# One attention step for each chunk between the first large products: next scores, output, state, in place of two half steps

## The chip, the cores and the metric

The kernel runs on one core of a Trainium2 chip. The metric is the device time of one execution in microseconds (us), lower is better. A profile is one execution recorded by the hardware profiler; its span runs from the first to the last instruction.

Five engines work side by side, each through its own queue in order: PE (TensorE, matrix products), DVE (VectorE), ACT (ScalarE), POOL (GpSimd) and SP (SyncE, which here issues the loads). They wait for each other through semaphores.

## What is computed

Three parts in a row, all in float32 (2 batches, 8 heads, 768 positions, 64 channels a head; 1536 tokens of 512 features afterwards):

```python
# 1: attention with decay, block by block, with a running state for each head
intra = (q_b @ k_b.T * Dmask) @ v_b
inter = (q_b * lam ** (pos + 1)) @ state
out_b = intra + inter
state = lam ** block * state + (k_b * lam ** (block - 1 - pos)).T @ v_b
# 2: first feed-forward
h = x @ w_in                      # 512 -> 2048
g = where(h >= 1, h, where(h <= -1, 0, (h + 1) ** 2 / 4))
x = g @ w_out
# 3: second feed-forward
x = ((x @ w_a) * (x @ w_b)) @ w_out2   # 512 -> 1536 -> 512
```

## The kernel before

The attention works on chunks of 128 positions, twelve of them (six for each batch; `CPB` is 6). Chunk `c` goes through four functions:

- `att_scores(c)`: eight small products of keys and queries on PE (line 131), into two PSUM banks.
- `att_mask(c)`: POOL scales the keys (`kd`, line 143) and the queries (`qd`, line 160), DVE multiplies the scores by the decay mask into two tiles `pm` (line 152).
- `att_state(c)`: eight products of `kd` and values on PE (line 173); POOL lets the old state decay (line 185) and DVE adds the new part (line 188; for the first chunk of a batch a copy, line 183). The last chunk of a batch (5 and 11) needs none.
- `att_out(c)`: state times `qd` (line 199, not for the first chunk of a batch) and values times `pm` (line 203) on PE into one bank. ACT and DVE write the result as a rounded part and a rest (lines 215 and 216) into `x`, which the first large product reads.

All large products go through `mm3` (line 277): float32 values stand as two rounded parts, so each product is three matmuls. The tokens are worked on in three blocks of 512, four chunks each, kept as `x` and later `y`. `h_bank(j, block)` is a product of twelve matmuls with its activation: ACT starts it (296), DVE goes on (297, 298), and ACT and POOL split it into the two parts of `g` (288, 289). Weights come as 64-bit numbers and are turned into two parts on the core by `split_w`: ACT (256, 260), DVE (257, 261, 264, 267), ACT and POOL again (288, 289).

Chunks 0 to 3 come first, in an order written out by hand. The scores and the mask of chunk 4 follow. From there a list of half steps is worked off between the first large products, two half steps after each `h_bank` of blocks 0 and 1, and three after the fourth. A half step is either "scores of the next chunk, state of this one" or "mask of the next chunk, output of this one, loads of the one after". Chunks 4 to 7 make `x` of block 1, which the fifth `h_bank` reads; chunks 8 to 11 make `x` of block 2. Outside the part written by hand, a scheduler sets the order of instructions on each engine at build time. Where the text says bank 0, 1, ... it means the `h_bank` calls in their order: 0 to 3 read block 0, 4 to 7 block 1.

Of the kernel before, what the change touches and what calls it, by code (L numbers as in the profile page):

```python
# [18 lines left out]
NCHUNK = B * S // CH  # L19
# [15 lines left out]
def retention_ffn_kernel(ctx: ExitStack, tc: tile.TileContext, lam, att, w1i, w1o, w2ab, w2o, out):  # L35
# [18 lines left out]
    def bank():  # L54
        return ps_p.tile([128, 512], F32, tag="ps", name="ps")

    def t2(name):
        return t2_p.tile([128, 512], F32, tag="t2", name=name)
# [55 lines left out]
    ck = {}  # L114
    sc = {}
    pm = {}
    kd = {}
    qd = {}

    def load_chunk(c, parts=(0, 1, 2, 3)):  # L120
        t = ck.setdefault(c, [None] * 4)
        for i in parts:
            t[i] = acc_p.tile([128, 512], F32, tag="acc", name=("qT", "kT", "kn", "vn")[i])
            nc.sync.dma_start(out=t[i], in_=att[c, i])

    def att_scores(c):
        qT, kT = ck[c][:2]
        sc[c] = [bank(), bank()]
        for h in range(H):
            p0, pr = 64 * (h % 2), h // 2  # L130
            nc.tensor.matmul(  # L131
                out=sc[c][h % 2][:, pr * CH:(pr + 1) * CH],
                lhsT=kT[p0:p0 + 64, pr * CH:(pr + 1) * CH],
                rhs=qT[p0:p0 + 64, pr * CH:(pr + 1) * CH],
                start=True,
                stop=True,
            )

    def att_mask(c):
        cc = c % CPB  # L140
        if cc < CPB - 1:
            kd[c] = t2("kd")
            (nc.vector if c == 0 else nc.gpsimd).tensor_tensor(  # L143
                out=kd[c].rearrange("p (a e d) -> p a e d", a=H // 2, e=2),
                in0=ck[c][2].rearrange("p (a e d) -> p a e d", a=H // 2, e=2),
                in1=dmask[:, :, CH - 1:CH].rearrange("p (a e) i -> p a e i", e=2).to_broadcast([128, H // 2, 2, D]),
                op=ALU.mult,
            )
        pm[c] = []
        for i in range(2):  # L150
            p = t2("pm")
            nc.vector.tensor_tensor(  # L152
                out=p.rearrange("p (a i) -> p a i", a=H // 2), in0=sc[c][i].rearrange("p (a i) -> p a i", a=H // 2),
                in1=dmask.rearrange("p (a e) i -> p e a i", e=2)[:, i], op=ALU.mult,
            )
            pm[c].append(p)
        del sc[c]
        if cc:
            qd[c] = t2("qd")
            (nc.vector if c == 3 else nc.gpsimd).tensor_tensor(  # L160
                out=qd[c], in0=ck[c][0], in1=tabq.rearrange("p a i -> p (a i)"), op=ALU.mult
            )

    def att_state(c):
        cc = c % CPB
        if cc == CPB - 1:
            return
        u = bank()
        k = kd.pop(c)

        for h in range(H):
            p0, pr = 64 * (h % 2), h // 2
            nc.tensor.matmul(  # L173
                out=u[p0:p0 + 64, pr * D:(pr + 1) * D],
                lhsT=k[:, h * D:(h + 1) * D],
                rhs=ck[c][3][:, h * D:(h + 1) * D],
                start=True,
                stop=True,
            )
        u4 = u[:, 0:H // 2 * D].rearrange("p (a e) -> p a e", a=H // 2)  # L180
        old, new = st[cc % 3], st[(cc + 1) % 3]
        if cc == 0:
            nc.vector.tensor_copy(new, u4)
        else:
            nc.gpsimd.tensor_tensor(
                out=new, in0=old, in1=tabq[:, :, CH - 1:CH].to_broadcast([128, H // 2, D]), op=ALU.mult
            )
            nc.vector.tensor_tensor(out=new, in0=new, in1=u4, op=ALU.add)

    def att_out(c):  # L190
        cc = c % CPB
        o = bank()
        s = st[cc % 3]
        pairs = [(pr, slice(pr * 128, (pr + 1) * 128)) for pr in range(H // 2)]
        if cc:
            for pr, cols in pairs:
                for e in range(2):
                    r = slice(64 * e, 64 * e + 64)
                    nc.tensor.matmul(out=o[r, cols], lhsT=s[r, pr, :], rhs=qd[c][r, cols], start=(pr == 0), stop=False)  # L199
        for pr, cols in pairs:  # L200
            for e in range(2):
                h = 2 * pr + e
                nc.tensor.matmul(  # L203
                    out=o[64 * e:64 * e + 64, cols],
                    lhsT=ck[c][3][:, h * D:(h + 1) * D],
                    rhs=pm[c][e][:, pr * CH:(pr + 1) * CH],
                    start=(cc == 0 and pr == 0),
                    stop=(pr == H // 2 - 1),
                )
        nb, t0 = c // 4, (c % 4) * CH  # L210
        if nb not in xy:
            xy[nb] = xy_p.tile([128, 2, KT, TB], F32R, tag="xy", name="x")
        o4 = o.rearrange("p (a i) -> p a i", a=KT)
        hi, lo = (xy[nb][:, i, :, t0:t0 + CH] for i in range(2))
        nc.scalar.copy(hi, o4)  # L215
        nc.vector.tensor_tensor(out=lo, in0=o4, in1=hi.bitcast(F32), op=ALU.subtract)  # L216
        for d in (ck, pm, qd):
            d.pop(c, None)


# [72 lines left out]
    def h_bank(ft, nb):  # L293
        ps = product_in("1i", ft, nb)
        r = t2("r")
        nc.scalar.activation(out=r, in_=ps, func=ACTF.Relu, scale=0.5, bias=half)  # L296
        nc.vector.scalar_tensor_tensor(out=r, in0=r, scalar=1.0, in1=r, op0=ALU.min, op1=ALU.mult)  # L297
        nc.vector.tensor_tensor(out=r, in0=r, in1=ps, op=ALU.max)
        g = g_p.tile([128, 2, 512], F32R, tag="g", name="g")
        split_act(r, g[:, 0], g[:, 1])  # L300
        gt[1, ft, nb] = g

    def ab_bank(ft, nb):
        pa = product_in("2i", 2 * ft, nb)
        a = t2("a")
        nc.scalar.copy(a, pa)  # L306
        pb = product_in("2i", 2 * ft + 1, nb)
        nc.vector.tensor_tensor(out=a, in0=a, in1=pb, op=ALU.mult)
        g = g_p.tile([128, 2, 512], F32R, tag="g", name="g")
        split_act(a, g[:, 0], g[:, 1])  # L310
        gt[2, ft, nb] = g
# [39 lines left out]
    with tc.manual_schedule(engines={mybir.EngineType.SP, mybir.EngineType.PE}):  # L351
# [19 lines left out]
        att_state(0)  # L371
        att_mask(1)
        att_out(0)
        att_state(1)
        att_scores(3)
        att_mask(2)
        att_out(1)
        att_state(2)
        split_w()
        att_mask(3)  # L380
        att_out(2)
        att_state(3)
        load_chunk(4)
# [4 lines left out]

    att_scores(4)
    att_mask(4)  # L390
    queue = [(c, half_way) for c in range(4, NCHUNK) for half_way in range(2)]

    def att_step():
        if not queue:
            return
        c, half_way = queue.pop(0)
        if not half_way:
            if c + 1 < NCHUNK:
                att_scores(c + 1)
            att_state(c)  # L400
        else:
            if c + 1 < NCHUNK:
                att_mask(c + 1)
            att_out(c)
            if c + 2 < NCHUNK:
                load_chunk(c + 2)

    def ahead(used):

        while nxt["split"] < min(used, len(order)):  # L410
            split_w()
# [4 lines left out]
    def second(s):  # L416
        f, g, nb = s
        last = g == (FF1 // 512 if f == 1 else FF2 // 256) - 1
        for m in range(4):
            if f == 1:  # L420
                y_bank(g, nb, m, last)
            else:
                o_bank(g, nb, m, last, 2 if last and nb == NB - 1 and m == 3 else 1)
            extra()
# [3 lines left out]
    def extra():  # L428
        if todo:
            todo.pop(0)()  # L430

    for i, s in enumerate(stages):
        f, g, nb = s
        if f == 1:
            base = 8 * g
            plan = {0: base + 7, 1: base + 10, 2: base + 12}
        else:
            base = 8 * (FF1 // 512) + 6 * g
            plan = {0: base + 6, 1: base + 8, 2: base + 10}
        need = plan[nb]  # L440
        if i == 0:
            ahead(4)
        todo.extend([split_w] * max(0, need - nxt["split"] - len(todo)))
        if f == 1:
            for j in range(4):
                h_bank(4 * g + j, nb)
                for _ in range(3 if (i, j) == (0, 3) else 2):
                    att_step()
                extra()
        else:  # L450
            for j in range(2):
                ab_bank(2 * g + j, nb)
                extra()
        if i:
            second(stages[i - 1])
# [47 lines left out]
```

## Time and profile before

| | |
|---|---|
| median of 3 runs | 631.24 us (629.97, 631.24, 631.33) |
| profiled execution | 629.82 us, span 628.0 us |
| mean granted clock of PE in it | 0.988 of full |
| PE busy | 610.6 us, 97% of the span |
| DVE, ACT, POOL busy | 375.7, 247.6, 246.5 us |

The shares are those of the whole span. The attention with the first large products lies in its first 92 us.

### The profile page before, as it was taken

Reading aid. Unit: us, or ns where it says so; the run is one execution under the profiler, and the core shown is the slowest. Engines: PE = TensorE matmul, PEld = TensorE weight load, DVE = VectorE, ACT = ScalarE, POOL = GpSimd, SP = SyncE. Lnnn points to the kernel's source line nnn. Section 1 sums busy time; section 2 is a strip of 40 time slices with the busy share of each in tenths; the row PEclk is TensorE's granted clock in tenths of the full one; section 3 lists DMA queues with packets and bytes.
Section 4 is the critical chain, followed back from the end, with each engine's and each line's share of the span. In section 5 each row is a group of like instructions: output and inputs, shape, how many; then the busy total and the mean of one; then the engine's idle time right before and its main releaser. Section 6 shows DMA issues by size and latency. Waiting matters only on the chain.

```text
span 628.0 us, 8231 instructions
## 1 busy us (share of the span) xinstructions
PE 610.6 (97%) x3171; PEld 501.9 (80%) x3172; DVE 375.7 (60%) x558; ACT 247.6 (39%) x421; POOL 246.5 (39%) x196
## 2 busy tenths in 40 slices
PE   5889899999999999999999999999999999999998
PEld 2768678888888888888888888888888888888886
DVE  0899792585787788679743333555555555555324
ACT  0344344455345435435453455333333333333110
POOL 1756662443352454335675333333322223333210
PEclk9899899999999999999999999999999999999999
DMA  6997210211111122123111221111121111210013
GB/s 192 390 335 261 64 63 24 68 67 68 67 68 55 67 80 68 33 68 101 52 49 34 68 67 68 67 68 67 68 68 67 55 57 58 67 34 1 1 67 135
DMA packets 20503, 52.71 MB, mean 84 GB/s; under 512 B 2408, under 2 KB 4208, under 8 KB 20464
## 3 DMA queue, kind: packets, MB, share of 16 engines
q1 hardware_dynamic: 20448, 52.18, 24.3%
q8 instruction: 25, 0.41, 0.3%
q14 instruction: 14, 0.11, 0.1%
q10 hardware_dynamic: 16, 0.00, 0.0%
HBM read 49.02 MB, written 3.15 MB: 83 GB/s over the span
## 4 chain that ended last, share of the span: by engine, by line
PE 93%; DMA 3%; DVE 2%; POOL 1%; issue 1%; ACT 0%; SPq 0%; DVEq 0%; POOLq 0%
PE ps L277 89%; PE ps L203 2%; PE ps L199 1%; PE ps L131 1%; DMA raw<-in_w1i 1%; DMA tabq<-rows 1%; DMA lamp<-in_lam 1%; PE ps L173 1%; DMA rows<-base 0%; POOL base L90 0%; DVE pm L152 0%; DVE v L261 0%; POOL kd L143 0%; POOL qd L160 0%; DVE x L216 0%
## 5 line engine op out<-in xcount | busy, mean ns | idle before, releaser
L277 PE MATMUL ps<-y,win 128*128 128x512 f32 x864 | 198.8, 389 | 0.0
L277 PEld LDWEIGHTS ps<-y,win 128*128 128x128 f32 x864 | 162.2, 188 | 33.6
L277 PE MATMUL ps<-x,win 128*128 128x512 f32 x576 | 137.1, 396 | 2.3 <-ACT x L215 1.8
L277 PE MATMUL ps<-g,wout 128*128 128x512 f32 x576 | 132.6, 389 | 0.0
L277 PEld LDWEIGHTS ps<-x,win 128*128 128x128 f32 x576 | 109.0, 190 | 26.6 <-ACT x L215 1.9
L277 PEld LDWEIGHTS ps<-g,wout 128*128 128x128 f32 x576 | 108.1, 188 | 22.5 <-issue 0.2
L289 POOL TENSOR_TENSOR win<-v,win 128x512 fp32r<-128x512 f32 x40 | 52.7, 1317 | 151.0 <-ACT win L288 151.0
L277 PE MATMUL ps<-wout,g 128*128 128x512 f32 (+1 forms) x438 | 100.7, 386 | 0.0
L289 POOL TENSOR_TENSOR g<-r,g 128x512 fp32r<-128x512 f32 x48 | 66.5, 1385 | 86.1 <-ACT g L288 60.8
L257 DVE TENSOR_SCALAR hc<-hc 128x512 f32<-128x512 f32 x68 | 36.9, 542 | 102.2 <-ACT hc L256 102.2
L277 PEld LDWEIGHTS ps<-wout,g 128*128 128x128 f32 x438 | 81.6, 188 | 16.7
L321 DVE TENSOR_TENSOR acc<-acc,ps 128x512 f32<-128x512 f32 (+1 forms) x97 | 64.8, 679 | 47.6 <-PE ps L277 47.5
L289 POOL TENSOR_TENSOR wout<-v,wout 128x512 fp32r<-128x512 f32 x28 | 36.7, 1312 | 85.2 <-ACT wout L288 85.0
L264 DVE SCALAR_TENSOR_TENSOR v<-raw,v 128x512 int32<-128x512 int32 x68 | 68.0, 1000 | 2.2
L297 DVE SCALAR_TENSOR_TENSOR r<-r 128x512 f32<-128x512 f32 x48 | 37.7, 786 | 50.3 <-ACT r L296 50.2
L267 DVE CUSTOM_DVE_ANT_0 v<-v,c 128x1024 uint16<-128x1024 uint16 x68 | 55.6, 818 | 6.3
L306 ACT COPY a<-ps 128x512 f32<-128x512 f32 x36 | 21.1, 587 | 95.3 <-PE ps L277 94.0
L288 ACT CAST win<-v 128x512 fp32r<-128x512 f32 x40 | 24.9, 621 | 84.7 <-DVE v L267 84.7
L289 POOL TENSOR_TENSOR g<-a,g 128x512 fp32r<-128x512 f32 x36 | 46.5, 1291 | 25.8 <-ACT g L288 25.8
L296 ACT ACTIVATE r<-ps,half 128x512 f32<-128x512 f32 x48 | 32.8, 684 | 47.2 <-PE ps L277 47.2
L261 DVE TENSOR_SCALAR v<-hc 128x512 int32<-128x512 int32 x68 | 44.5, 654 | 4.3
L256 ACT ACTIVATE hc<-raw 128x512 f32<-128x512 f32 x68 | 45.3, 665 | 2.0 <-DMA raw<-in_w1i 2.0
(45 smaller groups left out, 375.2 us busy)
## 6 DMA issues: line engine op xcount, KB each, us to landing
raw<-in_w2ab SPq DMA_DIRECT2D x24, 512.0 KB, 3.2
raw<-in_w1i SPq DMA_DIRECT2D x16, 512.0 KB, 3.3
raw<-in_w1o SPq DMA_DIRECT2D x16, 512.0 KB, 3.3
raw<-in_w2o SPq DMA_DIRECT2D x12, 512.0 KB, 3.4
qT<-in_att SPq DMA_DIRECT2D x12, 256.0 KB, 4.8
kT<-in_att SPq DMA_DIRECT2D x12, 256.0 KB, 5.0
kn<-in_att SPq DMA_DIRECT2D x12, 256.0 KB, 5.5
vn<-in_att SPq DMA_DIRECT2D x12, 256.0 KB, 5.7
```

Of the source, the lines that this page charges most:

```text
L256: nc.scalar.activation(out=hc.bitcast(F32), in_=high.bitcast(F32), func=ACTF.Abs)
L257: nc.vector.tensor_scalar(out=hc.bitcast(F32), in0=hc.bitcast(F32), scalar1=HIGH_MIN, scalar2=HIGH_MAX, op0=ALU.max, op1=ALU.min)
L261: nc.vector.tensor_scalar(out=v, in0=hc, scalar1=3, scalar2=0x3FFFFFFF, op0=ALU.logical_shift_left, op1=ALU.bitwise_and)
L264: nc.vector.scalar_tensor_tensor(out=v, in0=high, scalar=-0x40000000, in1=v, op0=ALU.bitwise_and, op1=ALU.bitwise_or)
L267: nc.vector.tensor_tensor(out=v, in0=v, in1=c, op=ALU.add)
L277: nc.tensor.matmul(out=ps, lhsT=l[a], rhs=r[b], start=(i == 0 and j == 0), stop=(i == n - 1 and j == 2))
L288: nc.scalar.copy(hi, src)
L289: nc.gpsimd.tensor_tensor(out=lo, in0=src, in1=hi.bitcast(F32), op=ALU.subtract)
L296: nc.scalar.activation(out=r, in_=ps, func=ACTF.Relu, scale=0.5, bias=half)
L297: nc.vector.scalar_tensor_tensor(out=r, in0=r, scalar=1.0, in1=r, op0=ALU.min, op1=ALU.mult)
L306: nc.scalar.copy(a, pa)
L321: nc.vector.tensor_tensor(out=total, in0=total, in1=ps, op=ALU.add)
```

## The change

The list holds one entry for each chunk from 4 to 11 in place of two, and one entry is worked off after each `h_bank`. Within it the order is: scores of the next chunk, output of this one, state of this one, mask of the next, loads of the one after. As the state now comes after the output, the output no longer drops the chunk's tiles from the dictionary `ck`.

```diff
@@ att_out
-        for d in (ck, pm, qd):
+        for d in (pm, qd):
             d.pop(c, None)
@@
-    queue = [(c, half_way) for c in range(4, NCHUNK) for half_way in range(2)]
+    queue = list(range(4, NCHUNK))
 
     def att_step():
         if not queue:
             return
-        c, half_way = queue.pop(0)
-        if not half_way:
-            if c + 1 < NCHUNK:
-                att_scores(c + 1)
-            att_state(c)
-        else:
-            if c + 1 < NCHUNK:
-                att_mask(c + 1)
-            att_out(c)
-            if c + 2 < NCHUNK:
-                load_chunk(c + 2)
+        c = queue.pop(0)
+        if c + 1 < NCHUNK:
+            att_scores(c + 1)
+        att_out(c)
+        att_state(c)
+        if c + 1 < NCHUNK:
+            att_mask(c + 1)
+        if c + 2 < NCHUNK:
+            load_chunk(c + 2)
@@
                 h_bank(4 * g + j, nb)
-                for _ in range(3 if (i, j) == (0, 3) else 2):
-                    att_step()
+                att_step()
                 extra()
```

PE's queue of before, from the scores of chunk 8 through the state and the output of chunk 7, the scores of chunk 9 and the state of chunk 8 to bank 4 and the output of chunk 8 (`st_93` to `st_95` are the three buffers that the state goes round in):

```order
L131 MATMUL ps<-qT,kT 128x128 x8
L173 MATMUL ps<-vn,kd 64x64 x8
L199 MATMUL ps<-qd,st_94 64x128 x8
L203 MATMUL ps<-pm,vn 64x128 x8
L131 MATMUL ps<-qT,kT 128x128 x8
L173 MATMUL ps<-vn,kd 64x64 x8
L277 MATMUL ps<-x,win 128x512 x12
L199 MATMUL ps<-qd,st_95 64x128 x8
```

The same place on PE now, from the scores of chunk 8 to the state of chunk 8:

```order
L131 MATMUL ps<-qT,kT 128x128 x8
L199 MATMUL ps<-qd,st_94 64x128 x8
L203 MATMUL ps<-pm,vn 64x128 x8
L173 MATMUL ps<-vn,kd 64x64 x8
L277 MATMUL ps<-x,win 128x512
L131 MATMUL ps<-qT,kT 128x128 x5
L277 MATMUL ps<-x,win 128x512 x11
L131 MATMUL ps<-qT,kT 128x128 x3
L199 MATMUL ps<-qd,st_95 64x128 x8
L203 MATMUL ps<-pm,vn 64x128 x8
L173 MATMUL ps<-vn,kd 64x64 x8
```

The state of chunk 7 stands behind its output, the scores of chunk 9 lie partly after the first matmul of bank 4 and partly behind the bank, and the state of chunk 8 stands behind the output of chunk 8.

DVE's queue of before, from the first operation of the weight split that lies ahead of `x` of chunk 7, through `x` of chunk 6 (the first L216) to `x` of chunk 7 (the last row):

```order
L257 TENSOR_SCALAR hc<-hc 128x512
L261 TENSOR_SCALAR v<-hc 128x512
L216 TENSOR_TENSOR x<-ps,x 128x4x128
L264 SCALAR_TENSOR_TENSOR v<-raw,v 128x512
L267 ISA v<-v,c 128x1024
L297 SCALAR_TENSOR_TENSOR r<-r 128x512
L298 TENSOR_TENSOR r<-r,ps 128x512
L152 TENSOR_TENSOR pm<-ps,dmask 128x512
L188 TENSOR_TENSOR st_95<-st_95,ps 128x256
L152 TENSOR_TENSOR pm<-ps,dmask 128x512
L216 TENSOR_TENSOR x<-ps,x 128x4x128
```

The same place on DVE now:

```order
L257 TENSOR_SCALAR hc<-hc 128x512
L216 TENSOR_TENSOR x<-ps,x 128x4x128
L261 TENSOR_SCALAR v<-hc 128x512
L264 SCALAR_TENSOR_TENSOR v<-raw,v 128x512
L267 ISA v<-v,c 128x1024
L297 SCALAR_TENSOR_TENSOR r<-r 128x512
L298 TENSOR_TENSOR r<-r,ps 128x512
L152 TENSOR_TENSOR pm<-ps,dmask 128x512 x2
L188 TENSOR_TENSOR st_95<-st_95,ps 128x256
L216 TENSOR_TENSOR x<-ps,x 128x4x128
```

`x` of chunk 6 stands ahead of L261, and both masks of chunk 8 stand ahead of the add. On POOL, at the same place, `qd` of chunk 7 now stands ahead of the split of `g` of bank 2, where it stood behind it.

DVE's queue of before between the adds of the states of chunk 9 and chunk 10 (first and last row):

```order
L188 TENSOR_TENSOR st_94<-st_94,ps 128x256
L267 ISA v<-v,c 128x1024
L152 TENSOR_TENSOR pm<-ps,dmask 128x512 x2
L297 SCALAR_TENSOR_TENSOR r<-r 128x512
L257 TENSOR_SCALAR hc<-hc 128x512
L298 TENSOR_TENSOR r<-r,ps 128x512
L216 TENSOR_TENSOR x<-ps,x 128x4x128
L261 TENSOR_SCALAR v<-hc 128x512
L264 SCALAR_TENSOR_TENSOR v<-raw,v 128x512
L188 TENSOR_TENSOR st_95<-st_95,ps 128x256
```

And now, between the adds of the same two states:

```order
L188 TENSOR_TENSOR st_94<-st_94,ps 128x256
L267 ISA v<-v,c 128x1024
L297 SCALAR_TENSOR_TENSOR r<-r 128x512
L298 TENSOR_TENSOR r<-r,ps 128x512
L152 TENSOR_TENSOR pm<-ps,dmask 128x512 x2
L257 TENSOR_SCALAR hc<-hc 128x512
L261 TENSOR_SCALAR v<-hc 128x512
L264 SCALAR_TENSOR_TENSOR v<-raw,v 128x512
L216 TENSOR_TENSOR x<-ps,x 128x4x128
L188 TENSOR_TENSOR st_95<-st_95,ps 128x256
```

The same operations stand between the two adds; the two masks moved behind the relu pair (L297, L298), and `x` behind the split's L264.

## Rows read from the trace of the kernel before

**Rows 1.** The page's first part: busy us, share of the span, instructions.
```profile
PE 610.6 (97%) x3171; PEld 501.9 (80%) x3172; DVE 375.7 (60%) x558; ACT 247.6 (39%) x421; POOL 246.5 (39%) x196
```
**Rows 2.** Busy time of all engines, 36.0 to 91.5 us: us, busy by engine, clock, DMA.
```profile
36.00:91.50 55.50, 50.80 (x534) 40.18 (x533) 50.60 (x71) 23.90 (x41) 35.20 (x30) 0.94 0.51 175
```
**Rows 3.** PE's waits: line and releaser, us in total, times, longest.
```profile
PE ps L199 <- POOL qd L160: 2.2, 1, 2.2
...
PE ps L277 <- ACT x L215: 1.8, 1, 1.8
```
**Rows 4.** PE's timeline: start, us, operation, idle before it and releaser.
```profile
61.93 1.16 PE L131 MATMUL ps<-qT,kT 64*128 64x128 f32 x16
63.02 0.69 PE L173 MATMUL ps<-vn,kd 128*64 128x64 f32 x16
65.49 0.51 PE L277 MATMUL ps<-x,win 128*128 128x512 f32 x1 [1.78 <-ACT x L215]
66.48 4.38 PE L277 MATMUL ps<-x,win 128*128 128x512 f32 x11 [0.49 <-DVE x L216]
...
77.49 1.09 PE L199 MATMUL ps<-qd,st 64*64 64x128 f32 x16
...
79.53 1.16 PE L131 MATMUL ps<-qT,kT 64*128 64x128 f32 x16
80.88 0.69 PE L173 MATMUL ps<-vn,kd 128*64 128x64 f32 x16 [0.19 <-POOL kd L143]
81.50 3.02 PE L277 MATMUL ps<-x,win 128*128 128x512 f32 x12
84.45 1.09 PE L199 MATMUL ps<-qd,st 64*64 64x128 f32 x16
```
**Rows 5.** PE in two stretches: us, PE busy, granted clock, DMA share, GB/s.
```profile
46.75:50.10 3.35, 3.35 (x26) 0.50 0.54 174
...
67.25:70.60 3.35, 3.35 (x9) 0.50 0.02 5
```
**Rows 6.** DVE's timeline between the adds of the states of chunks 9 and 10.
```profile
76.34 0.41 DVE L188 TENSOR_TENSOR st<-st,ps 128x256 f32<-128x256 f32 x1
76.67 0.68 DVE L267 CUSTOM_DVE_ANT_0 v<-v,c 128x1024 uint16<-128x1024 uint16 x1
77.27 1.28 DVE L152 TENSOR_TENSOR pm<-ps,dmask 128x512 f32<-128x512 f32 x2
78.63 1.28 DVE L297 SCALAR_TENSOR_TENSOR r<-r 128x512 f32<-128x512 f32 x1
79.83 1.27 DVE L257 TENSOR_SCALAR hc<-hc 128x512 f32<-128x512 f32 x1
...
82.68 1.66 DVE L264 SCALAR_TENSOR_TENSOR v<-raw,v 128x512 int32<-128x512 int32 x1
84.26 0.41 DVE L188 TENSOR_TENSOR st<-st,ps 128x256 f32<-128x256 f32 x1
```
**Rows 7.** Four lines of DVE over the whole span: shortest, median, longest in ns.
```profile
L257 DVE TENSOR_SCALAR hc<-hc x68: 411/428/1516, 22.7 to 579.9; 128x512 f32<-128x512 f32 x68
...
L261 DVE TENSOR_SCALAR v<-hc x68: 410/428/1516, 23.7 to 580.6; 128x512 int32<-128x512 int32 x68
...
L264 DVE SCALAR_TENSOR_TENSOR v<-raw,v x68: 691/693/1771, 25.0 to 581.1; 128x512 int32<-128x512 int32 x68
...
L297 DVE SCALAR_TENSOR_TENSOR r<-r x48: 677/680/1772, 39.0 to 314.4; 128x512 f32<-128x512 f32 x48
```
**Rows 8.** POOL's timeline, the split beside L264.
```profile
82.44 1.35 POOL L289 TENSOR_TENSOR g<-r,g 128x512 fp32r<-128x512 f32 x1 [0.18 <-ACT g L288]
```
**Rows 9.** The timelines of DVE and ACT ahead of the fifth bank.
```profile
58.72 1.38 DVE L261 TENSOR_SCALAR v<-hc 128x512 int32<-128x512 int32 x1
60.02 0.68 DVE L216 TENSOR_TENSOR x<-ps,x 128x512 fp32r<-128x512 f32 x1
...
64.86 0.58 ACT L215 CAST x<-ps 128x512 fp32r<-128x512 f32 x1
```

## The prediction

> **What bounds the kernel now.** I began with the page's busy shares: TensorE (PE) is busy 610.6 of 628.0 us [rows 1], so a change can win or lose here only where PE stands still or its clock is low. The list of PE's waits says where that is: behind the start-up, four waits, all in the attention of chunks 4 to 11: 2.2 us for the scaled query `qd` of chunk 5, 1.8 and 0.5 us for the two halves of `x` of chunk 7, 0.2 us for a `kd` [rows 3, 4]. The busy time of every engine over that stretch, 36.0 to 91.5 us, shows who PE waits for: VectorE (DVE) is busy 50.60 of 55.50 us, as long as PE, POOL 35.20, ACT 23.90 [rows 2]. In this stretch DVE sets the pace as much as PE does. Last come PE's timeline [rows 4], the granted clock [rows 5] and DVE's timeline [rows 6], for the prices.
>
> Two things are to be seen in them. First, one step of DVE, from the add of one state (76.34) to the next (84.26), takes 7.92 us [rows 6]. It holds one part of everything: two masks, the relu pair, one weight split, an `x`, an add. Second, a PE wait of some 2.2 us costs more than itself. After the 2.2 us for `qd` and after the 1.8 + 0.5 us for `x`, the clock stands at 0.50 of 2.4 GHz, that is 1.2 GHz, from 46.75 to 50.10 and from 67.25 to 70.60 [rows 5]. In the second stretch eleven products took 4.38 us [rows 4]; a whole bank of twelve takes 84.45 - 81.50 = 2.95 us, so eleven take 2.70. One such wait costs about 1.7 us more through the clock, and I use 1.6.
>
> **The change part by part.** No instruction is added or removed on any engine, SP keeps its order of loads, and all up to chunk 4's output stays. From PE's rows: scores are 63.02 - 61.93 = 1.09 us, a state 81.50 - 80.88 = 0.62, an output 79.53 - 77.49 = 2.04 [rows 4].
>
> *Chunk 5.* POOL's order up to `qd` of chunk 5 is the same and so is what feeds it, so the 2.2 us and their low clock stay: 0.
>
> *The third half step after bank 3 is gone.* Before, PE did the scores of 9 and the state of 8 (1.09 + 0.62 = 1.71 us) before it came to the first product of block 1 and waited for `x` of chunk 7. Now the state of 8 and three eighths of the scores stand behind that product's bank, and five eighths between its first and second matmul. If `x` comes when it came, PE waits 1.7 us longer; the five scores (0.68) fill the 0.5 us gap between the halves of `x` and overrun it by 0.2; the rest (0.41 + 0.62) is done behind: +1.2 us. But `x` should come earlier. ACT wrote its high half at 64.86, in a chain through DVE that starts with L261 at 58.72, which took 1.38 us where 0.41 is the shortest of its kind, and only then did DVE take `x` of chunk 6 (60.02, next start 0.60 later) [rows 7, 9]. Now `x` of 6 stands ahead of L261, inside the time that L261 is kept waiting, and `qd` of 7 ahead of a POOL split. That is worth 0.6, at most 0.9 us, against which stands that both masks of chunk 8 come ahead. I take +0.5; bounds +0.1 and +1.2. There is still a wait of over 2 us, so this low clock stays too.
>
> *The wait for `kd` of chunk 10* (0.2) goes, for the state of 10 now comes a whole output later: -0.2.
>
> *State behind output.* This is the main term. Before, an add of a state had a bank more to be ready in: the state of 10 ran at 80.88, its add began at 84.26, and PE wanted it only after two more banks and an output. Now the last three states are each wanted after one bank (and scores, while there are any). Take chunk 9. From the end of bank 5, PE does scores, output 9, state 9, bank 6 and scores, 1.09 + 2.04 + 0.62 + 2.95 + 1.09 = 7.8 us, and wants add 9. DVE needs the relu of bank 5, masks, split, `x` and the add: before, from the same bank's end (77.49) to the end of the next add (84.26 + 0.41) 7.2 us. So output 10 finds its state with 0.6 us to spare. From there PE has output 10, state 10 and bank 7, 2.04 + 0.62 + 2.95 = 5.6 us, and wants add 10, but DVE takes a full step, 7.92. The bare difference is a wait of 2.3 us at output 11, 1.7 with the 0.6 to spare. The order within DVE's step speaks for more: before, the two masks (77.27 to 78.55) lay between the add and the relu, while ACT finished the split and started the relu; now they stand behind the relu, and up to 1.2 us of DVE's wait for ACT is not filled: 2.9 us. I take 2.5. Bounds: in the step three operations took 0.60, 0.86 and 0.97 us longer than the shortest of their kind [rows 6, 7]; without these it is 5.5 us and the wait nothing. At the other end, no time to spare and the whole 1.2: 3.5.
>
> Those longer operations come from POOL. L264 at 82.68 ends at 84.34, 0.55 after POOL's split ended at 82.44 + 1.35 = 83.79 [rows 6, 8]. The Trainium skill (SBUF — State Buffer, "Who interferes with whom") states that a VectorE instruction with two SBUF inputs and a GpSimd instruction exclude each other, the later one blocked till the other ends. The trace agrees for L264, which sat out POOL's 1.35 us. By that rule L267, which also reads two SBUF tiles, would be kept waiting in the new order beside POOL; the sum by it is the third case below.
>
> *Clock behind the new wait.* 2.5 us is as long as the two waits that were followed by 1.2 GHz, so I add one such stretch: +1.6; bounds 0 and 1.7. It falls on the first products with `wout`.
>
> Sum: +0.5 - 0.2 + 2.5 + 1.6 = **+4.4 us** on the profiled execution's 629.82 (span 628.0): 634.2. The median of the runs shown is 631.24, 1.4 above that execution, and the three (629.97, 631.24, 631.33) lie as if one clock stretch more or less were in them. I put half of the 1.4 on top: **634.9 us**.
>
> **The rivals.** *Clock stays up.* The new wait comes as computed, but the clock does not follow: 634.9 - 1.6 = 633.3. For it: after the 0.2 us wait nothing fell. Against it: both long waits were followed by a fall.
>
> *DVE is held longer.* L267 is kept waiting by POOL at two places, in the chain to `x` of 7 (one operation's surplus, 0.97) and before add 9 (0.97 less the 0.6 to spare, so about 0.4 at output 10): 636.2. For it: the rule above. Against it: in the step shown L267 was not held (76.67 to 77.27).
>
> *No change.* DVE's step shrinks towards 5.5 us because POOL's operations fall elsewhere. From 5.6 + 0.6 = 6.2 us down output 11 doesn't wait, the clock stays, and only +0.5 - 0.2 is left: 630.1, with the same 0.7 on top 630.8. Against it: POOL's work per step is the same.
>
> *Faster.* On top of that the wait for `x` of 7 is cut in two by the five scores, the clock doesn't fall there, and `x` is 0.9 us earlier: 629.82 + 0.1 - 0.2 - 1.6 = 628.1, with 0.7 on top 628.8. The point that decides it is a DVE step of at most 6.2 us and a PE wait for `x` well under 2 us.
>
> **How the numbers follow.** Chances: my forecast 0.50, clock stays up 0.17, DVE held longer 0.17, no change 0.10, faster 0.06. The range leaves out the last two and reaches from 632.2 (clock up and a wait 1.1 us shorter) to 637.5 (the held case with the upper bound of the wait at output 11, 1 us more, and some clock). The difference that a measurement of this kernel can tell from none is about 0.2%, 1.26 us. Above 632.5 lie the first three cases but for a quarter of the second: slower 0.80; same 0.14; faster 0.06.
>
> **What would show it.** In the new profile PE's waits should list one for `st`, L188, of 1.7 to 2.9 us before the outputs of chunk 11, and a wait for `x` (L215) of 2.2 to 3.4 us, longer than the 1.8 before; the 2.2 us for `qd` of chunk 5 unchanged; a stretch at clock 0.50 soon after the new wait; and behind it the same pace of products. DVE's adds of the last two states should stand about 8 us apart. The prediction is wrong if no wait for `st` shows, if DVE's step is near 5.6 us, or if one of the old low stretches is gone.

## The result and the profile after

The changed kernel took 638.25 us (median of 4 runs, 636.63 to 639.28), the kernel before beside it 630.9 (629.97 to 631.33): 1.0121 times as long, 95% interval 1.0099 to 1.0142. That is slower, as forecast, but 3.35 us above the forecast 634.9 and above the range's end of 637.5. In the first experiment below the ratio was 1.0101 [1.0080, 1.0122], or 6.8 us. One run of `before_late2` further down (685.19 us, at a granted clock of 0.85) was in a slow state and is left out of its median.

The page's first line of the changed kernel shows the same work as [rows 1]:

```profile
PE 611.4 (96%) x3172; PEld 503.1 (79%) x3172; DVE 376.1 (59%) x558; ACT 247.7 (39%) x421; POOL 246.6 (39%) x196
```

PE is busy for 0.8 us more, in a span that is 9.5 us longer (637.5; this execution is the slowest of the four). So nearly all of the loss shows as waiting. Low clock adds to busy time too, but what came new at one place is offset by stretches that went elsewhere (behind `qd` of chunk 5, for one). Three lines of the list of PE's waits, beside [rows 3]:

```profile
PE ps L277 <- ACT x L215: 4.1, 1, 4.1
PE ps L199 <- DVE st L188: 3.8, 2, 2.8
PE ps L199 <- POOL qd L160: 2.9, 2, 2.4
```

The wait for `x` of chunk 7 went from 1.8 (and 0.5) to 4.1 us; two waits for a state are new, and so is one of 0.58 us for `qd` of chunk 7, the second in the last line. PE's timeline of the changed kernel, beside [rows 4]:

```profile
30.27 1.09 PE L199 MATMUL ps<-qd,st 64*64 64x128 f32 x16 [2.05 <-DVE qd L160]
...
48.17 1.09 PE L199 MATMUL ps<-qd,st 64*64 64x128 f32 x16 [2.36 <-POOL qd L160]
...
60.45 1.09 PE L199 MATMUL ps<-qd,st 64*64 64x128 f32 x16 [0.58 <-POOL qd L160]
...
67.09 0.79 PE L277 MATMUL ps<-x,win 128*128 128x512 f32 x1 [4.07 <-ACT x L215]
67.82 1.65 PE L131 MATMUL ps<-qT,kT 64*128 64x128 f32 x10
69.39 4.86 PE L277 MATMUL ps<-x,win 128*128 128x512 f32 x11
...
77.33 3.01 PE L277 MATMUL ps<-x,win 128*128 128x512 f32 x12
...
83.87 3.06 PE L277 MATMUL ps<-x,win 128*128 128x512 f32 x12
...
89.06 1.09 PE L199 MATMUL ps<-qd,st 64*64 64x128 f32 x16 [1.04 <-DVE st L188]
...
91.57 3.02 PE L277 MATMUL ps<-x,win 128*128 128x512 f32 x12
97.37 1.61 PE L199 MATMUL ps<-qd,st 64*64 64x128 f32 x16 [2.77 <-DVE st L188]
98.91 1.98 PE L203 MATMUL ps<-pm,vn 128*64 128x128 f32 x16
100.82 0.89 PE L277 MATMUL ps<-g,wout 128*128 128x512 f32 x2
```

The granted clock in three stretches of it (us, PE busy, clock, DMA share, GB/s), beside [rows 5]:

```profile
48.20:50.10 1.90, 1.90 (x32) 1.00 0.49 187
67.10:73.80 6.70, 6.70 (x21) 0.50 0.05 21
97.90:101.10 3.20, 3.20 (x28) 0.50 0.31 120
```

Behind the 2.36 us for `qd` of chunk 5 the clock did not fall this time. Behind `x` of chunk 7 it stood at 1.2 GHz for twice as long as before, and behind the new wait at output 11 it fell as forecast. DVE's timeline around the adds of the states of chunks 8, 9 and 10, beside [rows 6], with the operations that took longer than the shortest of their kind (and, for comparison, L267 at 88.83, which did not):

```profile
78.23 0.41 DVE L188 TENSOR_TENSOR st<-st,ps 128x256 f32<-128x256 f32 x1
78.56 1.21 DVE L261 TENSOR_SCALAR v<-hc 128x512 int32<-128x512 int32 x1
79.81 0.99 DVE L264 SCALAR_TENSOR_TENSOR v<-raw,v 128x512 int32<-128x512 int32 x1
80.83 1.43 DVE L267 CUSTOM_DVE_ANT_0 v<-v,c 128x1024 uint16<-128x1024 uint16 x1
...
85.93 1.33 DVE L261 TENSOR_SCALAR v<-hc 128x512 int32<-128x512 int32 x1
...
88.50 0.41 DVE L188 TENSOR_TENSOR st<-st,ps 128x256 f32<-128x256 f32 x1
88.83 0.68 DVE L267 CUSTOM_DVE_ANT_0 v<-v,c 128x1024 uint16<-128x1024 uint16 x1
90.79 1.28 DVE L297 SCALAR_TENSOR_TENSOR r<-r 128x512 f32<-128x512 f32 x1 [1.27 <-ACT r L296]
...
96.81 0.41 DVE L188 TENSOR_TENSOR st<-st,ps 128x256 f32<-128x256 f32 x1
```

The adds lie 10.3 and 8.3 us apart. The 1.43 us of L267 lie beside POOL's `kd`:

```profile
80.21 1.50 POOL L143 TENSOR_TENSOR kd<-kn,dmask 128x512 f32<-128x512 f32 x1
```

**Where the time went, stage by stage.** I count from the start of output 3, which lies ahead of everything that the change moves (28.18 us before, 30.27 after), and add 1.71 us (scores and a state) where the changed kernel has them still to do. Starts of before are those of [rows 4] and of these rows of the same timeline:

```profile
28.18 1.09 PE L199 MATMUL ps<-qd,st 64*64 64x128 f32 x16 [2.15 <-DVE qd L160]
...
86.49 3.02 PE L277 MATMUL ps<-x,win 128*128 128x512 f32 x12
89.44 1.09 PE L199 MATMUL ps<-qd,st 64*64 64x128 f32 x16
...
91.49 11.18 PE L277 MATMUL ps<-g,wout 128*128 128x512 f32 x48
```

| start of | before | after | after, at equal work | behind by |
|---|---|---|---|---|
| first product of bank 5 | 74.54 - 28.18 = 46.36 | 47.06 | 48.77 | 2.4 |
| bank 6 | 53.32 | 53.60 | 55.31 | 2.0 |
| bank 7 | 58.31 | 61.30 | 61.30 | 3.0 |
| output 11 | 61.26 | 67.10 | 67.10 | 5.8 |
| first product with `wout` | 63.31 | 70.55 | 70.55 | 7.2 |

So: 2.4 us around `x` of chunk 7, 1.0 at output 10, 2.8 at output 11, 1.4 by the clock behind it, 0.4 given back. The other 2.1 us between the two profiled executions lie ahead of output 3.

### The profile page after: what moved, and what is told of

It reads as the page before. It is cut to its first block, busy times and chain, and to the rows that moved or that the text cites. A ratio compares the mean times of both kernels' runs of the same rounds, so it can differ in the third digit from the quotient of the medians.

```text
span 637.5 us, 8223 instructions
## 1 busy us (share of the span) xinstructions
PE 611.4 (96%) x3172; PEld 503.1 (79%) x3172; DVE 376.1 (59%) x558; ACT 247.7 (39%) x421; POOL 246.6 (39%) x196
## 4 chain that ended last, share of the span: by engine, by line
PE 86%; DVE 9%; DMA 2%; issue 1%; ACT 1%; POOL 0%; SPq 0%; DVEq 0%
PE ps L277 85%; DVE v L264 1%; DVE v L261 1%; DVE pm L152 1%; DVE hc L257 1%; DMA dmask<-rows 1%; DVE r L297 1%; DVE v L267 1%; DVE x L216 1%; DMA lamp<-in_lam 1%; DVE r L298 1%; PE ps L203 1%; DMA rows<-base 0%; DVE st L188 0%; PE ps L173 0%
## 5 line engine op out<-in xcount | busy, mean ns | idle before, releaser
L289 POOL TENSOR_TENSOR wout<-v,wout 128x512 fp32r<-128x512 f32 x28 | 36.8, 1313 | 85.4 <-ACT wout L288 85.3
L297 DVE SCALAR_TENSOR_TENSOR r<-r 128x512 f32<-128x512 f32 x48 | 37.7, 785 | 53.3 <-ACT r L296 53.3
L264 DVE SCALAR_TENSOR_TENSOR v<-raw,v 128x512 int32<-128x512 int32 x68 | 66.1, 972 | 2.3
L267 DVE CUSTOM_DVE_ANT_0 v<-v,c 128x1024 uint16<-128x1024 uint16 x68 | 57.0, 838 | 6.7 <-DVE v L264 0.5
L261 DVE TENSOR_SCALAR v<-hc 128x512 int32<-128x512 int32 x68 | 44.6, 656 | 4.7 <-DVE hc L257 0.5
```

Of the source, the lines that this page charges most:

```text
L261: nc.vector.tensor_scalar(out=v, in0=hc, scalar1=3, scalar2=0x3FFFFFFF, op0=ALU.logical_shift_left, op1=ALU.bitwise_and)
L264: nc.vector.scalar_tensor_tensor(out=v, in0=high, scalar=-0x40000000, in1=v, op0=ALU.bitwise_and, op1=ALU.bitwise_or)
L267: nc.vector.tensor_tensor(out=v, in0=v, in1=c, op=ALU.add)
L289: nc.gpsimd.tensor_tensor(out=lo, in0=src, in1=hi.bitcast(F32), op=ALU.subtract)
```

## The experiments

Twelve kernels were measured, the first two without an edit. Below, "the stretch" is the time from the start of output 3 to the first product with `wout`: 63.31 us in the kernel before, 70.55 in the changed one.

| kernel | median us (runs) | ratio to before, 95% | stretch us |
|---|---|---|---|
| before, again | 631.44 (11) | 1.0006 [0.9997, 1.0015] | 63.29 |
| changed, again | 637.76 (6) | 1.0101 [1.0080, 1.0122] | 70.59 |
| state_first | 636.38 (4) | 1.0089 [1.0076, 1.0102] | 67.79 |
| third_kept | 635.42 (6) | 1.0071 [1.0058, 1.0084] | 66.40 |
| after_late_splits | 631.70 (11) | 1.0020 [1.0009, 1.0030] | 63.69 |
| after_no_scale | 634.07 (5) | 1.0059 [1.0047, 1.0072] | 66.67 |
| warm_out11 | 635.63 (5) | 1.0091 [1.0076, 1.0107] | 68.84 |
| after_warm | 634.66 (5) | 1.0069 [1.0056, 1.0082] | 66.22 |
| before_late_splits | 630.50 (11) | 0.9998 [0.9990, 1.0007] | 63.23 |
| state_first_late | 633.47 (6) | 1.0047 [1.0030, 1.0064] | 64.61 |
| after_late2 | 628.06 (5) | 0.9959 [0.9946, 0.9972] | 60.21 |
| before_late2 | 626.77 (5) | 0.9938 [0.9926, 0.9950] | 59.15 |

The kernel before, measured beside each of them, had medians of 630.34 to 630.96.

The first four expectations name theories 1 to 3: the change costs through PE's waits and the clock behind them (1), through a later start-up (2), or through the single step's order on DVE and what POOL does to it (3). The later ones name A to C, in the words of after_late_splits.

**Does the change delay the start-up?** Both kernels once more, unchanged.

> The kernel before, unchanged, for the spread of its start-up and of its low clock stretches. Theory 1 (the change costs through PE's waits and the clock behind them): time the same as before, and the start of the third output (28.2 us in the first profile) moves by 1 to 2 us from one profile to another with the landing of the first tables, so that the 2.1 us by which the changed kernel's profile was late there is no effect of the change. Theory 2 (the change delays the start-up itself): the start stays within 0.3 us of 28.2.

> The changed kernel, unchanged: 637 to 639 us. Theory 1: the third output's start lies anywhere between 28 and 30.5 us; the waits for x of chunk 7 (3.5 to 4.1 us) and for the states at outputs 10 and 11 (3.5 to 4 us together) come again. Theory 2: the third output starts at 30.3 us again.

Output 3 in the kernel before, again:

```profile
29.82 0.44 PE L199 MATMUL ps<-qd,st 64*64 64x128 f32 x4 [2.68 <-DVE qd L160]
```

and in the changed kernel, again:

```profile
29.45 0.76 PE L199 MATMUL ps<-qd,st 64*64 64x128 f32 x10 [2.28 <-DVE qd L160]
```

The one starts earlier in the changed kernel. The 2.1 us ahead of output 3 are a spread from execution to execution: over the profiles of these twelve it starts between 28.47 and 30.15 us. Theory 2 falls; the stretch behind it repeats to 0.1 us in each kernel and is what the change acts on.

**The two halves of the change, each alone.** state_first has one step for each chunk but the state ahead of the output:

```diff
-        att_out(c)
-        att_state(c)
+        att_state(c)
+        att_out(c)
```

> The changed kernel with the state put ahead of the output again; one step for each chunk stays. Theory 1 prices the state behind the output at 1.0 + 2.8 us of waits and 1.4 us of clock, 5.2 us: 633.0 us, no wait for st over 0.5 us, the wait for x of chunk 7 still 3 to 4 us. Theory 3 (the single step's order on DVE, where three operations collide with POOL, is what costs, whatever the place of the state): less than 2 us comes back, above 636 us.

third_kept has the output ahead of the state, but does the scores of 9 and the state of 8 ahead of bank 4, as the third half step did:

```diff
+        if c == 7:
+            att_scores(9)
+            att_state(8)
```

> The changed kernel with the scores of chunk 9 and the state of chunk 8 put back ahead of the first product of block 1 (the third half step of before); output before state stays elsewhere. Theory 1: the wait for x of chunk 7 falls from 4.1 to about 2 us and one of the two low clock stretches there goes, 2 to 2.5 us: 635.8 to 636.3 us; the waits for st at outputs 10 and 11 stay. Theory 3: no difference over 0.5 us, since DVE's order is nearly the same.

By the medians state_first costs 5.4 us, third_kept 4.5, both together 6.8, where 9.9 would be the sum. The halves share a loss. In third_kept `x` of chunk 7 costs nothing extra (waits of 1.49 and 0.49), but output 10 waits 1.17 us and output 11 2.79 us for the state, the latter with no low clock behind it in this execution:

```profile
92.82 1.09 PE L199 MATMUL ps<-qd,st 64*64 64x128 f32 x16 [2.79 <-DVE st L188]
93.84 1.09 PE L203 MATMUL ps<-pm,vn 128*64 128x128 f32 x16
```

In state_first the order that I blamed is gone, and output 11 still waits, for another input, with the clock falling behind it:

```profile
94.34 1.09 PE L199 MATMUL ps<-qd,st 64*64 64x128 f32 x16 [2.20 <-POOL qd L160]
95.36 1.97 PE L203 MATMUL ps<-pm,vn 128*64 128x128 f32 x16
```

So theory 1, which expected 633.0 of state_first, named the right wait in the changed kernel, but not what it takes to get rid of it: output 11 has lost its slack by either half. Theory 3 had the number (over 636). In third_kept it was the other way round: 635.42 lies just under the 635.8 to 636.3 of theory 1 and 2.3 us under the changed kernel, where theory 3 expected no difference over 0.5 us. Neither theory stands whole. Why output 11 still waits in state_first shows on ACT; bank 6 ended at 85.4, but its activation stood in ACT's queue behind a weight split that waited for DVE, and POOL's `qd` stood behind the split of that bank's `g`:

```profile
87.62 0.62 ACT L288 CAST win<-v 128x512 fp32r<-128x512 f32 x1 [3.74 <-DVE v L267]
88.15 0.68 ACT L296 ACTIVATE r<-ps,half 128x512 f32<-128x512 f32 x1
```

```profile
91.60 1.28 POOL L289 TENSOR_TENSOR g<-r,g 128x512 fp32r<-128x512 f32 x1 [2.00 <-ACT g L288]
92.84 1.45 POOL L160 TENSOR_TENSOR qd<-qT,tabq 128x512 f32<-128x512 f32 x1
```

**The weight split in DVE's step.** Two of the three splits of block 1 are moved behind its outputs, in the changed kernel, in state_first and in the kernel before:

```diff
-                extra()
+                if i != 1 or j == 0:
+                    extra()
```

> The changed kernel, with two of the three weight splits that lay between the products of block 1 moved behind its last output. Nothing of the computation is left out. Theory A (the state's add stands on DVE behind a weight split and everything that DVE does for it, so the step is as long as that): the waits for the state at the outputs of chunks 10 and 11 (1.0 and 2.8 us) go, and with them the clock behind the second (1.5): 637.8 - 5.3 = 632.5, 631.9 to 633.4; the wait for x of chunk 7 stays near 4.1. Theory B (what makes the step long is POOL holding up DVE, by kd, qd and the split of g, and not the weight split): the waits shrink by less than half, 636 or more. Theory C (the splits are wanted soon after): the waits go, but PE waits for wout or win behind the block, 635 or more.

> One step for each chunk with the state ahead of the output, as in state_first, and two weight splits of block 1 moved behind its outputs. In state_first the output of chunk 11 waited 2.2 us for qd, and in the changed kernel 2.8 us for the state. If both are the same thing, DVE's weight split of block 1, which ACT and POOL wait for in their queues too, the wait at output 11 and its clock go here as well: 636.4 - 2.2 - 1.6 = 632.6, 632.0 to 633.4, with the wait for x of chunk 7 left at 3.5 us. If the wait for qd comes from POOL's own load, it stays at over 1.5 us: 635.5 or more.

> The kernel before with two splits of block 1 moved behind its outputs. No PE wait of before hangs on these splits but the 0.2 us for kd, so theory A expects no difference: 630.3 to 631.5. If these splits cost anything by themselves, as load on DVE and POOL, it is faster by over 1 us; if they are wanted soon after, slower by over 1 us.

PE's timeline of after_late_splits: outputs 10 and 11 wait for nothing, and the products with `wout` start at full clock.

```profile
85.64 1.09 PE L199 MATMUL ps<-qd,st 64*64 64x128 f32 x16
...
91.14 1.09 PE L199 MATMUL ps<-qd,st 64*64 64x128 f32 x16
92.16 1.09 PE L203 MATMUL ps<-pm,vn 128*64 128x128 f32 x16
93.18 11.18 PE L277 MATMUL ps<-g,wout 128*128 128x512 f32 x48
```

Theory A holds: 631.70 where 631.9 to 633.4 was expected (a little better; in the profiled execution, at 631.50, only one low stretch followed `x` of chunk 7), and no wait appeared behind the block. In state_first_late the wait for `qd` went too, its stretch is 3.2 us shorter; its median of 633.47 stands just above the expected range. In the kernel before, the same edit is worth nothing. So these splits cost nothing as load; they cost only where the new order leaves no bank of slack between an add and its output.

**POOL beside DVE.** after_no_scale leaves out POOL's scaling of keys and queries for chunks 8 to 11.

> The changed kernel; it leaves out POOL's scaling of keys and queries of chunks 8 to 11 (the products read the keys and queries as they were loaded), so that POOL has seven operations less beside DVE's work for block 1. DVE, ACT and PE keep their order. Theory A: only what was held comes back, L267 and L257 in the step before add 9, about 1.3 us: the wait at output 10 (1.0) goes, the wait at output 11 stays at 2.3 to 2.8 us, 636.4 to 637.0. Theory B: the steps of DVE fall from 10.3 and 8.3 to under 7 us, both waits and the clock behind them go, 632.0 to 633.5.

DVE's timeline of it, between the same adds:

```profile
76.28 0.41 DVE L188 TENSOR_TENSOR st<-st,ps 128x256 f32<-128x256 f32 x1
...
78.88 0.69 DVE L267 CUSTOM_DVE_ANT_0 v<-v,c 128x1024 uint16<-128x1024 uint16 x1
...
83.23 0.43 DVE L261 TENSOR_SCALAR v<-hc 128x512 int32<-128x512 int32 x1
...
84.90 0.41 DVE L188 TENSOR_TENSOR st<-st,ps 128x256 f32<-128x256 f32 x1
...
93.21 0.41 DVE L188 TENSOR_TENSOR st<-st,ps 128x256 f32<-128x256 f32 x1
```

Without `kd` beside it L267 took 0.69 in place of 1.43 us. The second L261 took 0.43 in place of 1.33: without `qd` ahead of it, POOL's split of `g` ran earlier, and POOL was idle by then. The first step fell from 10.3 to 8.6 us and the wait at output 10 went; the second stayed at 8.3 and output 11 waited 2.05. As theory A has it, taking away POOL's holding is enough to end the wait at output 10, but not the one at output 11, which went only with the split. The time came out lower than A expected (634.07 for 636.4 to 637.0): `x` of chunk 7 was 0.6 us earlier too, since L267 ahead of it took 0.69 in place of 1.33, and no low clock followed the 2.05 in the profiled execution.

**The clock behind the waits.** warm_out11 puts ten products of zeros into the wait at output 11, after_warm fourteen more into the wait for `x` of chunk 7:

```diff
+                if (i, j) == (1, 0):
+                    warm(14)
                 h_bank(4 * g + j, nb)
...
+        if c == 11:
+            warm(10)
         att_out(c)
```

> The changed kernel with ten products of a tile of zeros on PE ahead of the output of chunk 11, inside the wait of 2.8 us; DVE and POOL keep their order. If the low clock behind that wait is a cost of its own (1.5 us: the output at 3.6 in place of 2.04): 636.3, with the output of chunk 11 at full clock and its start where it was. If the clock costs nothing there, or the idle products make the output later: 637.8 or more.

> The changed kernel with fourteen products of zeros ahead of the first product of block 1 (wait of 4.1 us for x of chunk 7) and ten ahead of the output of chunk 11. The five scores that lay inside the first bank of block 1 stand behind it. If the failed step of the sum is the clock behind x of chunk 7 (two stretches at 1.2 GHz in place of one, 3.2 us in all) and it is paid on the path: 637.8 - 3.2 - 1.5 = 633.1, at most 634.3. If DVE sets the pace whatever PE's clock is, the waits for the state at the outputs of chunks 10 and 11 grow by what the clock gives back: 636.3 or more, with waits of over 4 us there.

PE's timeline of after_warm:

```profile
61.83 3.20 PE L96 MATMUL ps<-idle 128*128 128x512 bf16 x14
65.97 0.50 PE L277 MATMUL ps<-x,win 128*128 128x512 f32 x1 [0.94 <-ACT x L215]
66.96 2.79 PE L277 MATMUL ps<-x,win 128*128 128x512 f32 x11 [0.49 <-DVE x L216]
...
85.02 1.09 PE L199 MATMUL ps<-qd,st 64*64 64x128 f32 x16 [1.00 <-DVE st L188]
...
93.32 1.09 PE L199 MATMUL ps<-qd,st 64*64 64x128 f32 x16 [0.61 <-DVE st L188]
```

`x` of chunk 7 came when it came before (36.82 us after output 3 in both), output 10 waited as long, and the eleven products behind `x` took 2.79 in place of 4.86 us: the clock was paid on the path. The stretch is 4.4 us shorter than in the changed kernel, in warm_out11 1.75. The times follow only in part. after_warm has 634.66 for the expected 633.1 to 634.3; its profiled execution is the fastest of its five, at 633.68. warm_out11 lies 1.5 us under the changed kernel by the medians, each set against the kernel before that was measured beside it, but its interval overlaps that of the changed kernel, so its price rests on the trace alone. Why the other executions took a microsecond more was not found.

**What sets `x` of chunk 7.** after_late2 and before_late2 also move a split out of block 0, the one that DVE works on ahead of that `x`. Block 0 then has two splits in place of three, block 1 two in place of three (behind its first and its second product), and two stand behind its outputs:

```diff
-                extra()
+                if (i, j) not in ((0, 2), (0, 3), (1, 2), (1, 3)):
+                    extra()
```

> The changed kernel with one weight split moved out of block 0 (the one that DVE works on ahead of x of chunk 7) into block 1 behind its second product, and one moved out of block 1 behind its outputs. If x of chunk 7 is paced by DVE's chain through that split: the wait for it falls from 4.1 to 1.0 to 1.9 us, and one or both stretches of low clock behind it go (1.6 to 3.2); the wait at output 11 (2.8) and its clock (1.5) go, that at output 10 (1.0) stays: 637.8 - 2.5 - 1.6 - 4.3 = 629.4, 628.0 to 630.5. If x of 7 is paced by something else, the wait stays near 4 us: 632 or more.

> The kernel before with the same two weight splits moved. If x of chunk 7 is paced by DVE's chain through the split, its wait (1.8 + 0.5 us) goes and the low clock behind it (1.6) too: 630.9 - 3.9 = 627.0, 626.3 to 628.2, and it beats both kernels. If the splits are only paid later (a new wait for a state or for wout in block 1, or for a weight behind it): 630 or more.

Bank 4 in before_late2:

```profile
64.06 0.69 PE L173 MATMUL ps<-vn,kd 128*64 128x64 f32 x16
64.68 3.02 PE L277 MATMUL ps<-x,win 128*128 128x512 f32 x12
```

No wait is left there and no low clock: 626.77 us, 4.1 less than the kernel before, and the fastest kernel of the study. In after_late2 `x` came 33.83 us after output 3 in place of 36.82, and the wait fell from 4.07 to 0.30; 628.06, where 628.0 to 630.5 was expected. Output 10 still waits (0.99). With the splits out of the way, the order that the change brings costs 1.3 us by the medians, in place of 6.8.

## Why the prediction was wrong

The direction was right, the size was not: +4.4 us on the profiled execution, where the stretch shows +7.2 (and the medians 6.8 to 7.35). Two steps failed.

**"There is still a wait of over 2 us, so this low clock stays too."** It came twice as long, from 67.1 to 73.8 us. The rest of the term of the third half step was right: `x` came 0.5 us earlier (36.82 for 37.31 after output 3; 0.6 forecast), the moved work cost +1.2, which makes +0.7; the other 1.7 of the 2.4 us fits 3.35 us more at half the clock. In after_warm the clock shows as a price of its own. The kernel after_late_splits, with the same wait of 4.07 us, had one low stretch only (eleven products in 3.50 in place of 4.86 us), so its length isn't fixed by the wait; what fixes it stays open.

**"So output 10 finds its state with 0.6 us to spare."** It waited 1.04 us. I took the 7.2 us from a step of the kernel before in which L267 was not held; in the new order it lies behind the end of bank 5, inside the time that counts, and beside `kd`, and L261 is held as well. That was the rival "DVE is held longer", and after_no_scale shows it. Both its places came true (at `x` of 7 L267 took 1.33 us, and leaving out the scaling brought `x` forward by 0.6); I had put 0.4 us on output 10, and the whole rival, at 636.2, had a chance of 0.17. The Trainium skill's rule that the prediction named there (SBUF — State Buffer, "Who interferes with whom") agrees with these rows: L267 took 0.69 us with POOL idle and 1.43 beside a `kd` of 1.50. L261 reads a single SBUF tile, so the rule as the prediction put it does not cover its 1.33 us.

What held: no instruction more; the wait for `kd` gone; the wait at output 11 (2.5 forecast, 2.77), DVE's step ahead of it (7.9 forecast, 8.3), the clock behind it (1.6 forecast, 1.4). That the size of the wait came so close is partly luck: the 0.6 us to spare that the 2.5 allowed for was not there, and of the up to 1.2 us for the order within DVE's step only 0.4 came (8.3 in place of 7.9 us). The cause given for that wait was too narrow. I put it on the state standing behind the output; state_first shows that the single step alone brings the same wait, through `qd`, because bank 6's activation stands behind a weight split on ACT. The two causes overlap, and the sum holds only for both together.

**"The 2.2 us and their low clock stay: 0."** The wait stayed (2.36), but the clock did not fall in the profiled execution, nor when the changed kernel was run again (2.35). That gave PE 1.5 us. A missing low stretch was one of the prediction's own signs of being wrong; why it is missing stays open. The gain was lost at once: `x` of chunk 7 came by DVE's chain and not by PE's, and PE only waited longer for it, 4.07 where at most 3.4 was forecast.

## What to carry to other kernels

Where PE and a helper engine are equally loaded, ask of each reordering how many products lie between an operation's start and its use, and what else stands in that helper's queue; here the change took the slack of one product, and a weight split that had cost nothing was then paid in full. Work with no near due time, like the splits, is best moved out of such a stretch: that was worth more (4.1 us) than any order of the attention steps tried. And time won on the engine that waits is not won, as long as the transfer or result it waits for comes at the same time.

## What the runs showed of the hardware

The granted clock after a wait of PE is not told by the wait's length. After 2.35 to 2.36 us for `qd` of chunk 5 it fell in third_kept and after_late2 and not in the changed kernel; after 2.79 us at output 11 it fell in the changed kernel, run again, and not in third_kept; the 1.8 + 0.5 us for `x` of chunk 7 were followed by 1.2 GHz in all three profiles that have them (the kernel before, twice, and before_late_splits).

The start-up varies by 1.7 us (28.47 to 30.15 at output 3) from execution to execution with the same program text ahead of it, more than some of the edits here are worth; a difference of two profiles is read from a point behind it.
